# The first batch of an attention-into-MLP kernel in a new order: exponentials over two PSUM banks, strided pairs first, local V ahead of the next loads

## The chip, the cores and the metric

The kernel runs on one core of one Trainium2 chip. The metric is the device time of one execution in microseconds; lower is better. The engines named below are TensorE (PE, with its weight loads PEld), VectorE (DVE), ScalarE (ACT), GpSimd (POOL) and the DMA queues, of which SP issues the hardware ones and POOL the software ones.

## The reference

Inputs are q, k, v of shape (8 batches, 8 heads, 576 positions, 64), and two weights, 512x2048 and 2048x512. Everything is given and returned as float32.

```python
scores = scale * np.matmul(q, k.transpose(0, 1, 3, 2))
rel = pos[:, None] - pos[None, :]
mask_local = (rel >= 0) & (rel < 32)
mask_strided = (rel >= 0) & (pos[None, :] % 32 == pos[:, None] % 32)
# heads 0..3 use mask_local, heads 4..7 mask_strided
attn = softmax(where(mask, scores, -1e9))
x = (attn @ v) as (4608 tokens, 512)       # heads side by side
h = x @ w_in; g = relu(h) ** 2; out = g @ w_out
```

## The kernel before

Attention and MLP are one program, interleaved by hand. The result of the attention, transposed, lies in four tiles `xt[0..3]` of 128 features by 4608 tokens: `xt[0]` and `xt[1]` take the local heads, `xt[2]` and `xt[3]` the strided ones. The MLP goes over nine chunks of 512 tokens. For each chunk, `mm1` makes 16 blocks of 128 hidden features, four 128x512 matmuls each (L662), then a ReLU on ACT (L668) and a square on DVE one tick later (L669); `mm2` makes 16 groups of four matmuls for the output (L684), copied by ACT and stored.

The order is written out. `BATCH0` is a string of words, run once at the start; `PLAN` gives words to be run ahead of numbered groups, a group being one `mm1` or `mm2` step of about 0.86 us of PE. The letter says what a word does: `c` casts loaded q or k to bf16, `T` transposes it on PE and copies it out of PSUM (last letter: a for ACT, v for DVE, g for POOL), `W` transposes strided rows, `S` scores and exponentials, `N` sums, logarithm and exponential for the reciprocal of the sum, `O` the product with V and the normalising multiplication (L609 for strided units), `D` the product with V and the normalisation of local units (L627, L628), `E` their transposition into `xt` (L644, L647), `H` a copy that shifts the rows of local V, `w` matmuls on zeros whose result nobody reads (L719), `P` the first three `mm1` blocks, with the feature tiles named after it, `m` a memset, `l`, `r`, `U`, `V`, `o` loads issued by POOL, `s` and `x` the scores and products of later strided heads (L562 and L568 are their multiplications). Units 0 and 1 of a batch are the local pairs of heads, 2 and 3 the strided ones; `c5q` is the cast of q for unit 5, that is unit 1 of batch 1.

Within one engine everything runs in the order in which the words issue it. The first batch uses PSUM through a rotating list of seven banks (`banks["b0"]`), a score step four of them: two halves by two rows (heads). In the first batch the mask is added on PE: a matmul puts a bias into the bank (L482) and the scores are accumulated on it (L493). Each of the four banks has an exponential of its own (L503). `step_N` takes the logarithm of each half by itself (L585) and then the exponential of both (L586).

The loads at the start are unit 0's q and k on SP, and on POOL, in order: strided q, strided k (with the construction of the identity between them), unit 1's q and k (L291), local V (L404), strided V (L572), the four slices of `w_in` (L425). Those on POOL share one software queue.

Of the kernel before, what the change touches and what calls it, by code (L numbers as in the profile page):

```python
# [12 lines left out]

FIRST = (0, 2, 3, 1)
NP = 3
BATCH0 = """
    c0qv c0ka T0qa c1kg w2 T0kv S0 mk1v c1qv W0k0a w3 W0q0v W0k1a W0q1v T1qv w2 T1kv S2 S1 H0v D0.0 D0.1 S3
    D1.0 N3 D1.1 N2 E0a O3 O2 E1a w1 P0 P23 P1  # L20
"""
PLAN = """
0: l1q4+5 l1k4+5 z
1: r1q U1 mv1g
3: o0
4: r1k V1 mk0v
5: o1 l2k8+9 mbg
6: o2 o3 V2 mv0v
7: c4qv
8: c5qv  # L30
9: c4kv
10: l2q8+9 c5ka T4qa
11: T4kv T5qa
12: W1q0v T5ka
13: S4
14: W1q1v
16: W1k0a S5! B10v
17: W1k1a
18: D4.0 k10v mrg C2q C2k
19: k11v  # L40
20: D4.1 s1.0 B11v
21: D5.0 s1.1 U2
22: l3k12+13 s1.2
23: D5.1
24: E5v x1.0
26: X2k l3q12+13
27: E4v x1.1 c9kv
28: V3
29: x1.2 c8qv
30: c8ka c9qv  # L50
31: X2q
34: C3q B20v
35: T8kv B21v
37: T9kv
38: T8qv C3k
39: k20v
40: U3
41: S8! k21v
42: T9qa
44: S9! D8.0  # L60
46: D8.1
47: E8
# [101 lines left out]
def kernel(  # L164
# [41 lines left out]
    PS = bass.MemoryType.PSUM  # L206
    strTs = {nm: ctx.enter_context(tc.tile_pool(name=f"strT{nm}", bufs=n)) for nm, n in (("q", 2), ("k", 1))}
    psum = ctx.enter_context(tc.tile_pool(name="psum", bufs=1, space=PS))
    banks = {nm: [psum.tile([128, 512], FP32, name=f"{nm}{i}") for i in range(n)]
             for nm, n in (("ph", 2), ("py", 1), ("pt", 5))}  # L210

    banks["b0"] = banks["pt"] + banks["ph"]
    in_b0 = [True]

    def bank(nm):
        if in_b0[0] and nm == "pt":
            nm = "b0"
        t = banks[nm].pop(0)
        banks[nm].append(t)
        while id(t) in unread:  # L220
            run_due(lambda x: x[1] == unread[id(t)])
        return t

    unread = {}

# [219 lines left out]
        clock[0] += 1  # L445
        run_due(lambda x: x[0] <= clock[0])

    def step_T(u, name, copy):
        s = st[u]
        src = s[name].rearrange("p j h d -> p (j h d)")  # L450
        pt = bank("pt").bitcast(BF16)[:, 0:S]
        for j in range(6):
            nc.tensor.transpose(pt[:, QL * j:QL * (j + 1)], src[:, 128 * j:128 * (j + 1)],  # L453
                                ident[0:QL, 0:QL])
        if name == "k":
            full = kTl[v_slot(u)]
            dst = full[:, 32:32 + S]
        else:
            full = dst = qkT.tile([128, S], BF16, name="qT")
        copy(dst.rearrange("c (p j) -> c p j", j=6), pt.rearrange("c (j p) -> c p j", j=6))  # L460
        s[name + "T"] = full
# [4 lines left out]
    def step_S(u, mode=0):  # L466
        s = st[u]
        qT, kT = s["qT"], s["kT"]
        local = is_local(u)
        w, n = (QL, NL) if local else (SP_, NJ)  # L470
        kn = 128 if local else SP_
        hn = n // 2
        e = es[u % 4]
        s["e"] = e
        pss = [[None, None], [None, None]]
        for half in range(2):
            for row in range(2):
                pss[row][half] = bank("pt")
                if u < 4:
                    bias = bias_l[:, half].rearrange("p t c -> p (t c)") if local \  # L480
                        else bias_s.rearrange("p t c -> p (t c)")
                    nc.tensor.matmul(pss[row][half][0:kn, 0:S // 2], ident[0:kn, 0:kn], bias,  # L482
                                     start=True, stop=False, skip_group_check=True)
            for i in range(hn):
                t = half * hn + i
                klo = w * t
                for row in range(2):
                    rows = slice(64 * row, 64 * row + 64)
                    if not local:
                        lhsT, rhs = (a[rows, t // 4, t % 4, :] for a in (kT, qT))  # L490
                    else:
                        lhsT, rhs = kT[rows, klo:klo + kn], qT[rows, w * t:w * (t + 1)]
                    nc.tensor.matmul(pss[row][half][0:kn, w * i:w * (i + 1)], lhsT, rhs,  # L493
                                     start=u > 3, stop=True, skip_group_check=u < 4)

        for row in range(2):
            for half in range(2):
                unread[id(pss[row][half])] = u

        def expo(row, half):  # L500
            del unread[id(pss[row][half])]
            lo = S * row + S // 2 * half
            nc.scalar.activation(e[0:kn, lo:lo + S // 2], pss[row][half][0:kn, 0:S // 2],  # L503
                                 AF.Exp, scale=scale)

        def masks(row):
            x = e[0:kn, S * row:S * (row + 1)].rearrange("p (t c) -> p t c", c=w)
            m = mask_all if local else mask_str.to_broadcast([kn, n, w])
            nc.vector.tensor_tensor(x, x, m, op=ALU.mult)  # L509

        if u < 4:
            for half in range(2):
                for row in range(2):
                    expo(row, half)
            return
        if mode == 1:
            for row in range(2):
                for half in range(2):
                    expo(row, half)
                later(row + 1, lambda row=row: masks(row), u)  # L520
            return
        expo(0, 0)
        later(1, lambda: expo(0, 1), u)
        later(2, lambda: (masks(0), expo(1, 0)), u)
        later(3, lambda: expo(1, 1), u)
        later(4, lambda: masks(1), u)
# [17 lines left out]
    def step_XX(b, part):  # L544
# [11 lines left out]
        for h in (3,) if part == 2 else range(3):  # L556
            for par in range(2):
                r, x = slice(64 * par, 64 * par + 64), slice(64 * (h % 2), 64 * (h % 2) + 64)
                to = xt[2 + h // 2][x, b * S:(b + 1) * S].rearrange("c (m a r) -> c m a r", a=NP2, r=2)
                if part < 2:  # L560
                    of, by = (y[r, 0:W3 * n].rearrange("c (a h m) -> c h m a", a=n, h=3)[:, h] for y in (po, rv))
                    nc.vector.tensor_tensor(to[:, :, NJ * part:NJ * (part + 1), par], of, by, op=ALU.mult)  # L562
                    continue
                of, by = (y[r, 0:W3 * n].rearrange("c (a g m) -> c g m a", a=n, g=3) for y in (po, rv))
                for lo, g, k in ((0, 0, NG), (NG, 2, 1)):
                    t = to[:, :, 2 * NG * (g == 2) + lo, par]
                    t = bass.AP(t.tensor, t.offset, [t.ap[0], [2 * NG, 3 - g], [STRIDE, NA], [2, k]])
                    nc.vector.tensor_tensor(t, of[:, g:, :, lo:lo + k], by[:, g:, :, lo:lo + k], op=ALU.mult)  # L568

    def load_v0():  # L570
        load_v_local_sw(0)
        nc.gpsimd.dma_start(  # L572
            out=vs0.rearrange("p u n d -> p (u n d)").rearrange("p (h c) -> p h c", h=4),
            in_=v[0, 4:8].rearrange("h (p j) d -> p h (j d)", j=NJ))

    def step_N(u):
        e, hw = st[u]["e"], S // 2
        kn = 128 if is_local(u) else SP_
        for half in range(2):
            pn = bank("pt")  # L580
            for h in range(2):
                c = S * h + hw * half if is_local(u) else S * half + hw * h
                nc.tensor.matmul(pn[64 * h:64 * h + 64, 0:hw], ones[0:kn], e[0:kn, c:c + hw],
                                 start=True, stop=True)
            nc.scalar.activation(rv0[:, u, hw * half:hw * (half + 1)], pn[:, 0:hw], AF.Ln)  # L585
        nc.scalar.activation(rv0[:, u], rv0[:, u], AF.Exp, scale=-1.0)  # L586

    def step_O(u):
        s = st.pop(u)
        e, hw = s["e"], S // 2  # L590
        for half in range(2):
# [12 lines left out]
            for t in range(hw // w):  # L604
# [2 lines left out]
                    nc.tensor.matmul(po[64 * h:64 * h + 64, w * t:w * (t + 1)], vt, e[0:w, c:c + w],  # L607
                                     start=True, stop=True)
            nc.vector.tensor_tensor(  # L609
                xt[u][:, 0:S].rearrange("c (p j r) -> c p j r", j=NJ // 2, r=2)[:, :, :, half],  # L610
                po[:, 0:hw].rearrange("c (j p) -> c p j", p=SP_),
                rv.rearrange("c (j p) -> c p j", p=SP_), op=ALU.mult)

    def step_D(u, part):
        run_due(lambda x: x[1] == u)
# [105 lines left out]
    idle = xt[0][:, T - 512:T]  # L721

    def first_part(kks):
        in_b0[0] = False
        for ff in range(NP):
            mm1(0, ff, kks, FIRST, None if ff < 2 else "py")

    def run_step(word):
# [3 lines left out]
        elif op == "c":  # L732
            cast_qk_local(int(arg[:-2]), arg[-2], ENG[arg[-1]])
        elif op == "T":
            step_T(int(arg[:-2]), arg[-2], ENG[arg[-1]])
        elif op == "W":
            step_TS(int(arg[0]), arg[1], int(arg[2]), ENG[arg[3]])
        elif op == "S":
# [65 lines left out]
    def memset_later(which, eng):  # L804
# [5 lines left out]
        else:  # L810
# [3 lines left out]
    nc.scalar.preload_act_table_set("natural_log_exp_and_others")  # L814
    load_qk_hw(0)
    load_str_rows(0, "q")
    make_identity(nc, ident)
    load_str_rows(0, "k")
    nc.vector.memset(idle, 0.0)
    nc.vector.memset(mask_loc, 1.0)  # L820
    warm(8)
    nc.vector.memset(ones, 1.0)
    nc.vector.memset(kTl[0][:, 0:32], 0.0)
    nc.vector.memset(kTl[1][:, 0:32], 0.0)
# [19 lines left out]
    nc.vector.memset(bias_l[0:32, 0, 0], -NEG)  # L844
    nc.vector.tensor_scalar(bias_s, mask_str.to_broadcast([SP_, NJ // 2, SP_]),
                            NEG, -NEG, op0=ALU.mult, op1=ALU.add)
    load_qk_local_sw(0, (1,))
    load_v0()
    for i in range(4):
# [75 lines left out]
```

## Time and profile before

| | us |
|---|---|
| median of three runs (304.8 to 307.27) | 307.2 |
| the profiled execution | 307.11 |
| its span in the trace | 305.4 |
| PE busy | 297.6 (97%) |
| DVE busy | 179.7 (59%) |
| ACT busy | 173.2 (57%) |
| POOL busy | 73.3 (24%) |

Busy times are sums over the span; a busy PE is not PE at its peak. The lines of the span's first 60 us that the prediction works with stand there. Times in the trace start at the span's start.

### The profile page before, as it was taken

How to read it: one execution, taken by the hardware profiler on the slowest of the kernel's cores; microseconds unless marked ns; L12 is line 12 of the kernel's file. 1: busy time of each engine (PE TensorE's matmuls, PEld its weight loads, DVE VectorE, ACT ScalarE, POOL GpSimd, SP SyncE). 2: the span in 40 equal slices, each digit the busy share in tenths (PEclk: the TensorE clock that was granted, in tenths of full speed). 3: DMA queues.
4: the chain of work that ended last, by engine and by line, in shares of the span. 5: the costliest groups of instructions: out<-in, count | busy, mean ns of one | idle time of the engine just before them, and what ended most of it. 6: DMA issues, size and time to landing. Idle time of an engine off the chain costs nothing.

```text
span 305.4 us, 5745 instructions
## 1 busy us (share of the span) xinstructions
PE 297.6 (97%) x2177; PEld 147.8 (48%) x2177; DVE 179.7 (59%) x465; ACT 173.2 (57%) x342; POOL 73.3 (24%) x105
## 2 busy tenths in 40 slices
PE   7989899999999999999999999999999999999996
PEld 3554455455554544454445444444454444444444
DVE  4675777888578776575558394685576525104400
ACT  3395763768658754674477455744675446216611
POOL 8745835008131044066100840000000000000000
PEclk9999999999999999999999999999999999999999
DMA  8999999999989989599977998811110110010012
GB/s 149 184 206 195 188 201 189 161 202 138 144 137 205 134 156 188 125 151 150 199 123 125 136 181 175 118 21 71 69 23 19 71 70 0 34 71 34 0 69 71
DMA packets 93643, 37.28 MB, mean 122 GB/s; under 512 B 78956, under 2 KB 87750, under 8 KB 93616
## 3 DMA queue, kind: packets, MB, share of 16 engines
q0 software_dynamic: 54960, 18.82, 55.8%
q1 hardware_dynamic: 38512, 18.03, 29.7%
q8 instruction: 17, 0.28, 0.4%
q14 instruction: 10, 0.08, 0.1%
q10 hardware_dynamic: 144, 0.07, 0.1%
HBM read 38.21 MB, written 9.44 MB: 156 GB/s over the span
## 4 chain that ended last, share of the span: by engine, by line
PE 90%; DVE 5%; ACT 2%; issue 2%; POOL 0%; DVEq 0%; ACTq 0%; POOLq 0%
PE ph L662 38%; PE ph L684 36%; PE pt L493 2%; PE pt L622 2%; PE pt L453 2%; DVE xt L562 2%; PE pt L538 1%; PE pt L552 1%; PE ph L709 1%; PE pt L549 1%; PE py L719 1%; PE py L684 1%; DVE g_sb L669 1%; PE pt L482 1%; PE pt L684 1%
## 5 line engine op out<-in xcount | busy, mean ns | idle before, releaser
L662 PE MATMUL ph<-xt,w_in_b 128*128 128x512 bf16 x568 | 131.9, 379 | 1.1 <-ACT xt L647 0.8
L684 PE MATMUL ph<-w_out_b,g_sb 128*128 128x512 bf16 x528 | 121.1, 379 | 0.1
L668 ACT ACTIVATE r<-ph 128x512 bf16<-128x512 f32 x142 | 84.8, 599 | 35.2 <-PE ph L662 31.2
L669 DVE TENSOR_TENSOR g_sb<-r 128x512 bf16<-128x512 bf16 x144 | 60.5, 422 | 64.6 <-ACT r L668 63.8
L662 PEld LDWEIGHTS <-w_in_b 128*128 128x128 bf16 x576 | 53.0, 97 | 59.7 <-issue 2.3
L684 PEld LDWEIGHTS <-g_sb 128*128 128x128 bf16 x560 | 51.7, 98 | 57.4 <-DVE g_sb L669 0.5
L688 ACT COPY y<-ph 128x512 f32<-128x512 f32 x33 | 19.4, 589 | 53.1 <-PE ph L684 53.1
L562 DVE TENSOR_TENSOR xt<-pt,rv 64x144 bf16<-64x144 f32 x84 | 34.0, 405 | 18.4 <-ACT rv L555 17.3
L503 ACT ACTIVATE e<-pt 128x288 bf16<-128x288 f32 (+1 forms) x68 | 24.1, 417 | 8.7 <-PE pt L493 8.5
L554 ACT ACTIVATE rv<-pt 128x432 f32<-128x432 f32 (+1 forms) x21 | 10.5, 501 | 13.8 <-PE pt L549 13.8
L628 DVE TENSOR_TENSOR x_l<-pt,rinv 96x384 bf16<-96x384 f32 x30 | 16.6, 554 | 1.0
L568 DVE TENSOR_TENSOR xt<-pt,rv 64x270 bf16<-64x270 f32 (+1 forms) x28 | 10.9, 432 | 8.1 <-ACT rv L555 8.0
L350 POOL DMA_DIRECT2D q_t<-in_q_dram x6 | 3.5, 591 | 47.0 <-DMA qT_s<-q_t 47.0
L509 DVE TENSOR_TENSOR e<-e,mask_all 128x576 bf16<-128x576 bf16 x28 | 12.4, 453 | 3.9 <-ACT e L503 3.5
L539 ACT ACTIVATE e<-pt 128x432 bf16<-128x432 f32 (+1 forms) x21 | 10.4, 497 | 6.6 <-PE pt L538 6.6
L279 POOL DMA_DIRECT2D k_l<-in_k_dram x16 | 12.0, 759 | 2.2 <-DMA v_st<-in_v_dram 1.2
L279 POOL DMA_DIRECT2D q_l<-in_q_dram x16 | 11.7, 732 | 2.0 <-DMA k_l<-in_k_dram 1.3
L622 PEld LDWEIGHTS <-e 128*128 128x128 bf16 x192 | 9.1, 97 | 5.8 <-issue 0.4
L419 POOL DMA_DIRECT2D vl<-in_v_dram x7 | 10.0, 1436 | 6.3 <-DMA vl<-in_v_dram 2.7
L555 ACT ACTIVATE rv<-rv 128x432 f32<-128x432 f32 (+1 forms) x21 | 11.2, 533 | 0.7
L350 POOL DMA_DIRECT2D k_t<-in_k_dram x6 | 3.2, 539 | 29.8 <-DMA kT_s<-k_t 29.8
L622 PE MATMUL pt<-vl,e 128*128 128x65 bf16 x180 | 9.9, 193 | 0.0
(130 smaller groups left out, 223.5 us busy)
## 6 DMA issues: line engine op xcount, KB each, us to landing
out_dram<-y SPq DMA_DIRECT2D x35, 256.0 KB, 3.6
vl<-in_v_dram POOLq DMA_DIRECT2D x7, 384.0 KB, 9.4
w_in_b<-in_moe_w_in_dram POOLq DMA_DIRECT2D x4, 512.0 KB, 12.8
w_out_b<-in_moe_w_out_dram POOLq DMA_DIRECT2D x4, 512.0 KB, 13.9
q_t<-in_q_dram POOLq DMA_DIRECT2D x7, 288.0 KB, 6.8
k_t<-in_k_dram POOLq DMA_DIRECT2D x7, 288.0 KB, 5.9
v_st<-in_v_dram POOLq DMA_DIRECT2D x7, 216.0 KB, 7.5
k_l<-in_k_dram POOLq DMA_DIRECT2D x16, 72.0 KB, 6.7
```

Source lines behind the costliest of these rows:

```text
L279: nc.gpsimd.dma_start(out=t[:, :, hh, :], in_=src[b, 2 * p + hh].rearrange("(t p) d -> p t d", p=QL))
L503: nc.scalar.activation(e[0:kn, lo:lo + S // 2], pss[row][half][0:kn, 0:S // 2], AF.Exp, scale=scale)
L509: nc.vector.tensor_tensor(x, x, m, op=ALU.mult)
L555: nc.scalar.activation(rv, rv, AF.Exp, scale=-1.0)
L562: nc.vector.tensor_tensor(to[:, :, NJ * part:NJ * (part + 1), par], of, by, op=ALU.mult)
L622: nc.tensor.matmul(po[:, n, :], e[:, c:c + 128], rhs[:, NL * part + n, 0:D + 1], start=True, stop=True)
L628: nc.vector.tensor_tensor(x, po[0:QL, :, 0:D], rinv[0:QL].to_broadcast([QL, NL, D]), op=ALU.mult)
L662: nc.tensor.matmul(ph, w_in_b[:, kk, 128 * ff:128 * (ff + 1)], xt[kk][:, 512 * c:512 * (c + 1)], start=(kk == order[0]), stop=(kk == order ...
L668: nc.scalar.activation(r, ph, AF.Relu)
L669: later(1, lambda: nc.vector.tensor_tensor(g[:, ff, :], r, r, op=ALU.mult))
L684: nc.tensor.matmul(py, g[:, ff, 128 * j:128 * (j + 1)], w_out_b[:, ff, :], start=(ff == 0), stop=(ff == 15))
L688: nc.scalar.copy(y, py)
```

## The change

`BATCH0` is reordered. The strided units 2 and 3 are scored ahead of unit 1; unit 0's q is cast by ACT and its k by DVE; both casts of unit 1 are on DVE; the shift of local V is on POOL; unit 1's transposed k uses the bank that the spare matmuls use; unit 2's and unit 3's sums and products stand between the steps of units 0 and 1; there are ten spare matmuls at the start and 21 in all instead of 16; P takes feature tile 2 first and tiles 3 and 1 last (`FIRST`). The strided k load is issued ahead of the identity, local V ahead of unit 1's q and k. PSUM becomes one tile with eight slices, so that a score step in the first batch can take two neighbouring banks (`bank_pair`) and have one exponential over both rows of a half, and `step_N` one logarithm over both halves. In `PLAN` the words of batch 1 are moved, most by some groups; of the four memsets of the block tiles `kbds` and `vbds` (L812), one of `kbds`, so far on DVE in the first batch, is on POOL. The multiplications of `step_O` and `step_XX` go through their inputs in the order in which these lie, and write with the stride instead.

```diff
-FIRST = (0, 2, 3, 1)
+FIRST = (2, 0, 3, 1)
 BATCH0 = """
-    c0qv c0ka T0qa c1kg w2 T0kv S0 mk1v c1qv W0k0a w3 W0q0v W0k1a W0q1v T1qv w2 T1kv S2 S1 H0v D0.0 D0.1 S3
-    D1.0 N3 D1.1 N2 E0a O3 O2 E1a w1 P0 P23 P1
+    c0qa c0kv T0qa w1 T0kv w1 S0 W0q0v W0q1v w3 W0k0a W0k1v S2 H0g c1qv c1kv S3 T1qv w2 T1kvp D0.0 D0.1 N2 S1 O2 N3
+    E0a D1.0 D1.1 O3 w2 E1a w2 P2 P0 P31
 """
 PLAN = """
 0: l1q4+5 l1k4+5 z
-1: r1q U1 mv1g
+1: r1q U1 mk0v
+2: mk1g mv1g
 3: o0
-4: r1k V1 mk0v
-5: o1 l2k8+9 mbg
-6: o2 o3 V2 mv0v
-7: c4qv
-8: c5qv
-9: c4kv
-10: l2q8+9 c5ka T4qa
-11: T4kv T5qa
-12: W1q0v T5ka
-13: S4
-14: W1q1v
-16: W1k0a S5! B10v
-17: W1k1a
-18: D4.0 k10v mrg C2q C2k
-19: k11v
-20: D4.1 s1.0 B11v
-21: D5.0 s1.1 U2
-22: l3k12+13 s1.2
-23: D5.1
-24: E5v x1.0
-26: X2k l3q12+13
-27: E4v x1.1 c9kv
-28: V3
-29: x1.2 c8qv
+4: r1k o1 mv0v
+5: V1 mbg
+6: o2 o3
+7: l2k8+9 V2
+9: c4qv
+10: c5qv T4qa l2q8+9
+12: c4kv c5ka T5qa
+13: T4kv W1q0v
+14: T5ka W1q1v
+15: S4
+16: B10v
+17: W1k0a W1k1a
+18: S5!
+19: k10v mrg C2q C2k B11v
+20: k11v
+21: s1.0 U2
+22: s1.1 D4.0
+23: s1.2 D4.1 l3k12+13
+24: D5.0
+25: D5.1 x1.0
+26: E5v l3q12+13
+27: x1.1
+28: E4v V3
+30: x1.2 c9kv
...
-    banks = {nm: [psum.tile([128, 512], FP32, name=f"{nm}{i}") for i in range(n)]
-             for nm, n in (("ph", 2), ("py", 1), ("pt", 5))}
-
-    banks["b0"] = banks["pt"] + banks["ph"]
+    psb = psum.tile([128, 8, 512], FP32, name="psb")
+    all_banks = [psb[:, i] for i in range(8)]
+    banks = {"b0": all_banks[0:7], "py": all_banks[7:8], "ph": [], "pt": []}
...
+    def bank_pair():
+
+        order = [bank_no[id(t)] for t in banks["b0"]]
+        i = min(range(6), key=lambda i: max(order.index(i), order.index(i + 1)))
+        two = all_banks[i:i + 2]
+        banks["b0"] = [t for t in banks["b0"] if t is not two[0] and t is not two[1]] + two
+        return two, psb[:, i:i + 2]
...
+            if u < 4:
+                (pss[0][half], pss[1][half]), both = bank_pair()
...
+            if u < 4:
+                hw = S // 2
+                nc.scalar.activation(e[0:kn, 0:2 * S].rearrange("p (r c) -> p r c", r=2)[:, :, hw * half:hw * (half + 1)],
+                                     both[0:kn, :, 0:hw], AF.Exp, scale=scale)
+        if u < 4:
+            return
...
-        if u < 4:
-            for half in range(2):
-                for row in range(2):
-                    expo(row, half)
-            return
...
-                to = xt[2 + h // 2][x, b * S:(b + 1) * S].rearrange("c (m a r) -> c m a r", a=NP2, r=2)
+                to = xt[2 + h // 2][x, b * S:(b + 1) * S].rearrange("c (m a r) -> c a m r", a=NP2, r=2)
                 if part < 2:
-                    of, by = (y[r, 0:W3 * n].rearrange("c (a h m) -> c h m a", a=n, h=3)[:, h] for y in (po, rv))
-                    nc.vector.tensor_tensor(to[:, :, NJ * part:NJ * (part + 1), par], of, by, op=ALU.mult)
+                    of, by = (y[r, 0:W3 * n].rearrange("c (a h m) -> c h a m", a=n, h=3)[:, h] for y in (po, rv))
+                    nc.vector.tensor_tensor(to[:, NJ * part:NJ * (part + 1), :, par], of, by, op=ALU.mult)
...
     def load_v0():
-        load_v_local_sw(0)
         nc.gpsimd.dma_start(
...
-            nc.scalar.activation(rv0[:, u, hw * half:hw * (half + 1)], pn[:, 0:hw], AF.Ln)
+        r = rv0[:, u].rearrange("p (t c) -> p t c", t=2)
+        nc.scalar.activation(r, both[:, :, 0:hw], AF.Ln)
         nc.scalar.activation(rv0[:, u], rv0[:, u], AF.Exp, scale=-1.0)
...
-                xt[u][:, 0:S].rearrange("c (p j r) -> c p j r", j=NJ // 2, r=2)[:, :, :, half],
-                po[:, 0:hw].rearrange("c (j p) -> c p j", p=SP_),
-                rv.rearrange("c (j p) -> c p j", p=SP_), op=ALU.mult)
+                xt[u][:, 0:S].rearrange("c (p j r) -> c j p r", j=NJ // 2, r=2)[:, :, :, half],
+                po[:, 0:hw].rearrange("c (j p) -> c j p", p=SP_),
+                rv.rearrange("c (j p) -> c j p", p=SP_), op=ALU.mult)
...
     load_qk_hw(0)
     load_str_rows(0, "q")
+    load_str_rows(0, "k")
     make_identity(nc, ident)
-    load_str_rows(0, "k")
     nc.vector.memset(idle, 0.0)
     nc.vector.memset(mask_loc, 1.0)
-    warm(8)
+    warm(10)
...
+    load_v_local_sw(0)
     load_qk_local_sw(0, (1,))
     load_v0()
```

## The prediction

> **What bounds the kernel now.** I read the windows first, then the waits of PE, then the chain and the timeline of the first 35 us, then the DMA landings, last the groups by shape.
>
> ```profile
> 40.00:50.00 10.00, 9.50 (x107) 5.17 (x104) 7.79 (x22) 4.66 (x12) 4.52 (x7) 1.00 1.53 190
> 50.00:100.00 50.00, 49.74 (x414) 25.52 (x413) 38.96 (x100) 34.11 (x69) 13.14 (x18) 1.00 1.31 167
> 100.00:200.00 100.00, 100.00 (x722) 48.78 (x720) 66.00 (x171) 60.18 (x121) 28.99 (x39) 1.00 1.16 149
> ```
>
> Columns: window, length, then busy time of PE, PEld, DVE, ACT, POOL. From 60 us on PE lists no wait at all, so the matmuls alone set that stretch and nothing there can give or take. The rest is decided before 60 us:
>
> ```profile
> PE pt L453 <- DVE q_l L298: 1.7, 2, 1.1
> PE py L719 <- DVE xt L819: 1.3, 1, 1.3
> PE ph L662 <- ACT xt L647: 0.8, 1, 0.8
> PE pt L493 <- ACT e L503: 0.5, 1, 0.5
> ...
> PE ph L662 <- DVE xt L568: 0.2, 1, 0.2
> ```
>
> ```profile
> 20.52 0.61 ACT g_sb L585 x2
> ...
> 21.74 0.63 ACT xt L647
> 22.37 0.04 issue
> 22.41 0.59 PE ph L662 x2
> ...
> 28.43 1.23 DVE kb L812
> ...
> 30.51 1.23 DVE vb L812
> ...
> 32.02 0.31 DVE q_l L298
> 32.33 0.05 issue
> 32.38 0.43 PE pt L453 x6
> ```
>
> The first dense stage starts at 22.41, when ACT has copied unit 0's output (L647). Its 12 matmuls of P end at 25.06; I call this instant T. PE then runs without a break to 31.26, waits 1.1 us for the cast of batch 1's q on DVE, which is behind two memsets of 1.23 us and seven squares of r, loses 0.5 us at S5 and 0.2 us at 59.46. So the time is T plus a fixed amount of matmul work plus those stalls, and I sum changes of T and of the stalls.
>
> ```profile
> 9.57 0.66 PE L332 MATMUL ph<-ident,w_out_b 96*128 96x96 bf16 x6
> 13.96 0.42 PE L453 MATMUL pt<-ident,k_l 96*128 96x96 bf16 x6
> ```
>
> Two sets of six 96-column transposes: the later set takes two thirds. The 128x512 spare matmuls follow each other after 0.43 us up to 13.6, the dense ones after 0.215 from 22.4. PE ran at half rate until about 13.8, although the granted clock column shows 1.00. Its unbroken stretch 1.27 to 4.87 (3.6 us) did not bring the short durations; the one from 8.27 (5.5 us, gaps under 0.1) did.
>
> **The change, part by part.** Start: ten spare matmuls at 0.427 reach 5.54. ACT casts q at its landing (0.82+3.4=4.2, 0.83 us, ready 5.1), DVE casts k (landing 1.28+3.8=5.1, 0.49 us, ready 5.6), so both transposes follow without a gap, with one spare each, to about 7.2. That is 5.9 us unbroken, more than the 5.5 that sufficed, so I take the short durations from about 7 us. Moving the strided k load ahead of the identity's construction costs 0.73 us of POOL, covered by those spares. The Trainium skill ("TensorE: Matmul & The Clock Gate", Part 1) says that about 3.4 us of sustained work in a free-running window lifts the gate; the 3.6 us stretch that failed fits a window that began before it, and by this rule too the switch comes by about 8 us.
>
> Loads: local V (2304 pieces) now goes ahead of unit 1's q and k.
>
> ```profile
> w_out_b<-in_k_dram POOLq DMA_DIRECT2D x1, 288.0 KB, 6.7
> vl<-in_v_dram POOLq DMA_DIRECT2D x1, 288.0 KB, 8.3
> xt<-in_q_dram POOLq DMA_DIRECT2D x1, 144.0 KB, 6.0
> xt<-in_k_dram POOLq DMA_DIRECT2D x1, 144.0 KB, 6.0
> ```
>
> Last column: us from issue to landing. Before: strided k 2.74+6.7=9.4, q1 4.25+6.0=10.3, k1 4.91+6.0=10.9, V 5.53+8.3=13.8. One queue serves them in order, so V now lands near 9.4+2.9=12.3 and k1 last of the five: at 13.8 at the latest by this, or near 12.7, as the small pieces' long tail no longer ends the group. I take 13.3, and 12.6 for q1. V's shift moves from DVE (0.49 us) to POOL, where it waits for V; by POOL's 96x768 copy (0.82 us) it takes an estimated 1.4, ready by 13.8. Behind it on POOL are batch 1's loads (issued at 11.78, now about 13.8); their data were behind w_in's last slice anyway (9.8+15.5=25.3), so nothing is late. The memset of kb that POOL takes over from DVE (1.29) delays w_out's first load by about 0.7, hidden by the same queue.
>
> Strided pairs first: with the fast clock their transposes, scores and exponentials fill PE until about 12.8, so unit 1 waits only for its load. From there DVE is the chain, in its new order: cast of k1 0.4, two transposed copies 0.75 each, two normalisations of unit 0 (0.19+0.55, pitch 0.72) 1.45, which free the bank that O2 needs, O2's matmuls 0.5, two products, then a 0.3 wait for unit 1's matmuls, two normalisations 1.45, E1's transposes 0.4, two spares 0.43:
> 13.3+0.4+1.5+1.45+0.5+0.9+0.3+1.45+0.4+0.4 = 20.6; P's 12 matmuls 2.65 give T=23.3. P31 needs the ACT copy of E1 (20.3+0.65=20.95) and O3 (21.1), both before P2 and P0 end at 21.9. T gains 1.8.
>
> ```profile
> L562 DVE TENSOR_TENSOR xt<-pt,rv 64x144 bf16<-64x144 f32 x84 | 34.0, 405 | 18.4 <-ACT rv L555 17.3
> L628 DVE TENSOR_TENSOR x_l<-pt,rinv 96x384 bf16<-96x384 f32 x30 | 16.6, 554 | 1.0
> L609 DVE TENSOR_TENSOR xt<-pt,g_sb 128x288 bf16<-128x288 f32 x2 | 1.2, 642 | 0.0
> ```
>
> Products of O: reading with a stride 288 columns cost 0.64, while 384 columns read in order cost 0.55. In order I estimate 0.45 each (L628's slope), 0.9 for two; if the write, now 16 or 64 bytes apart, costs what the read saved, 1.3. L562 would go from 0.405 to about 0.3, on an engine that has slack later. The Trainium skill ("Advanced Engine Details and Errata", Memory Cachelines) charges every access that lands in another 16-byte line, writes not excepted; by it the products stay at 0.64 and the sum rises by 0.4.
>
> Exponentials over two banks: eight of 576 columns for sixteen of 0.417; 576 columns cost 0.63 in L647, so ACT saves 8x0.2=1.6, and 0.3 on the Ln pairs. If two banks cost like two instructions nothing is saved: ACT would deliver E1 near 21, still ahead of 21.9. Zero on the chain either way. The spares rise from 16 to 21; only the last two (0.43) are on the chain, in the sum.
>
> Batch 1: the two DVE memsets stay ahead of c4q, and the cast now stands behind nine squares instead of seven. From the same T: seven squares end the before's wait at T+7.3. Two more cost 0.7, and P31's order gives the first r 0.43 earlier, of which I count 0.3: T4q at T+7.7, so 0.4 worse. c4k stands behind the square of group 11, and T4k only one group later: r 0.6, square 0.4, cast 0.4 and 0.2 of latencies against 0.86+0.26 of matmul work: a new wait of 0.45. S5 meets its banks as before. x1.2 comes one group later, against shorter products: between 0 and 0.5 for chunk 1's start, I take 0.1.
>
> Sum: -1.8+0.4+0.45+0.1 = -0.85. The profiled execution took 307.1 (span 305.4 and 1.7 around it), as much as the median of 307.2; so 306.2.
>
> **The rivals.**
> - The head wins more: k1 lands at 12.7 (-0.6) and DVE keeps up in batch 1, so that T4q waits for nothing (-1.5, the wait left in my sum) and T4k hardly (-0.4). For it: the memsets start earlier, l1q has landed at 11.78+15.0=26.8. Against: DVE's backlog is in the chain row by row. 303.7.
> - The load order bites: k1's landing decides from 14.15 on, where the 0.85 is gone. If it lands where the group behind it landed before (6.7+8.5=15.2), T is 25.2 and the batch 1 waits remain: 308.1, slower than before. For it: V's pieces are the slowest kind in that queue. Against: its bytes are fewer than all that had landed by 13.8.
> - PE stays at half rate to 13.8, because transposes are too thin to count: S3 ends near 14.9, T1k's copy at 16.8 instead of 15.2, T=24.9: 307.8. Against: the stretch that did end it held 24 transposes.
> - The single tile for all banks makes PE wait for strangers, so that the change doesn't do what it says. The built program has fewer waits on PE (454 against 463), so this has little: a wait of 0.1 at each of 35 output copies would give 309.7.
> - The write penalty above: 306.6, inside my case.
>
> **How the numbers follow.** 1% (3.1 us) is about what a measurement of this kernel can tell from no change. My case 0.53 with the penalty inside it, the head's win 0.24, load order 0.1, half rate 0.1, strangers 0.03. Within 1% are mine, load order and half rate, less what their tails cross; faster by over 1% needs a little more than the first rival, and the lowest of the runs before, 304.8, shows that an execution can lie 2.4 lower unaided. Faster 0.27, same 0.66, slower 0.07. Range: down to the first rival, past it a little, up past load order: 303.3 to 308.6.
>
> **What would show it.** Right: six-transposes at 0.42 from about 7 us on; unit 1's casts on DVE waiting for their DMA at 12.6 and 13.3; P's first matmul at 20.6; T4q waiting about 1.5 for DVE and T4k about 0.45; L562 near 0.3; nothing waiting on PE after 60 us. Wrong: P later than 22, transposes at 0.66 up to 13, or a DMA as PE's releaser between 25 and 60 us.

## The result and the profile after

| | median, us | lowest to highest | profiled execution | span |
|---|---|---|---|---|
| before, same chip | 306.16 | 304.8 to 307.27 | 307.11 | 305.4 |
| after | 335.33 | 333.88 to 336.79 | 336.79 | 335.1 |

The changed kernel takes 1.0955 times as long (95% interval 1.0867 to 1.1043): 29 us slower, where I had forecast 306.2 and a range that ended at 308.6.

The windows of after, with the columns of those shown for before (window, length, busy time of PE, PEld, DVE, ACT and POOL, granted clock, DMA):

```profile
20.00:25.00 5.00, 4.36 (x24) 1.81 (x25) 3.84 (x5) 0.64 (x1) 2.35 (x3) 0.70 1.26 206
40.00:50.00 10.00, 9.33 (x104) 4.88 (x104) 6.37 (x17) 6.42 (x16) 5.19 (x8) 1.00 1.55 190
50.00:100.00 50.00, 42.48 (x346) 21.78 (x350) 41.86 (x84) 27.56 (x53) 12.40 (x17) 0.97 0.94 133
100.00:200.00 100.00, 93.16 (x665) 45.29 (x678) 77.83 (x160) 55.85 (x113) 30.47 (x42) 1.00 1.13 140
```

Before, PE was busy for 49.74 and for all of 100.00 us in the last two windows. Now it stands still for 7.5 and 6.8 us in them, and DVE has grown from 38.96 to 41.86 and from 66.00 to 77.83 although fewer instructions ran. Little of the loss is in the head that the change is mostly about: P's first matmul starts at 22.09, just past the 22 that the prediction names as a sign of being wrong, and T is 26.3 instead of 25.06 (with the old multiplications, in the first experiment, 23.1). That is 1.3 of the 29.7 us between the two spans. Most of the rest is in the stretch that I had called settled. PE's waits say for whom:

```profile
PE psb L513 <- DVE xt L583: 5.5, 2, 3.9
PE psb L683 <- DVE xt L589: 3.7, 2, 2.0
PE psb L665 <- DVE xt L583: 2.5, 1, 2.5
PE psb L570 <- DVE xt L583: 2.4, 1, 2.4
PE psb L705 <- DVE g_sb L690: 2.3, 1, 2.3
PE psb L470 <- DVE q_l L315: 1.8, 1, 1.8
```

L583 and L589 are the multiplications of `step_XX` (L562 and L568 in before). Groups by shape on DVE (busy us, mean ns of one, idle time ahead of them):

```profile
L583 DVE TENSOR_TENSOR xt<-psb,rv 64x144 bf16<-64x144 f32 x84 | 66.0, 785 | 17.7 <-ACT rv L576 16.5
L589 DVE TENSOR_TENSOR xt<-psb,rv 64x270 bf16<-64x270 f32 x14 | 18.7, 1339 | 0.8 <-ACT rv L576 0.6
...
L630 DVE TENSOR_TENSOR xt<-psb,g_sb 128x288 bf16<-128x288 f32 x4 | 5.5, 1554 | 0.5 <-ACT e L517 0.5
```

Before, the same three shapes took 405, 634 and 642 ns; the prediction shows the first and the last, and this is the second:

```profile
L568 DVE TENSOR_TENSOR xt<-pt,rv 64x270 bf16<-64x270 f32 x14 | 8.9, 634 | 8.1 <-ACT rv L555 8.0
```

The 84 products of 144 columns alone cost DVE 32 us more. One place in the timeline shows how that reaches PE. DVE in before, then DVE and PE in after:

```profile
54.93 2.52 DVE L562 TENSOR_TENSOR xt<-pt,rv 64x144 bf16<-64x144 f32 x6 [0.28 <-ACT rv L555]
```

```profile
54.79 4.76 DVE L583 TENSOR_TENSOR xt<-psb,rv 64x144 bf16<-64x144 f32 x6 [0.56 <-ACT rv L576]
59.60 0.64 PE L665 MATMUL psb<-ident,x_l 96*128 96x96 bf16 x6 [2.55 <-DVE xt L583]
```

Six products in a row hold DVE for 4.76 us (before, 2.52). PE's next transposes need a PSUM bank that those products still read, and PE waits 2.55 us. And they then run as a set of six in 0.64, the half-rate length, not 0.42: after the pause the clock has gone down. The 0.70 in the window from 20 to 25 us is another such stretch, behind waits of 0.42, 0.96 and 0.45 us. In the trace's clock records after is at half rate at 21.97–25.39, 59.52–62.93, 202.88–209.71 and 233.6–237.0, together 17.1 us, in which at most half, 8.5 us, is lost.

### The profile page after: what moved, and what is told of

The parts are those of the page before. It is cut to its first block, busy times and chain, and to the rows that moved or that the text cites. A ratio compares the mean times of both kernels' runs of the same rounds, so it can differ in the third digit from the quotient of the medians.

```text
span 335.1 us, 5696 instructions
## 1 busy us (share of the span) xinstructions
PE 303.3 (91%) x2143; PEld 148.6 (44%) x2182; DVE 223.1 (67%) x465; ACT 173.0 (52%) x331; POOL 76.0 (23%) x106
## 4 chain that ended last, share of the span: by engine, by line
PE 63%; DVE 24%; ACT 5%; issue 4%; DMA 2%; POOL 1%; DVEq 0%; ACTq 0%; POOLq 0%
PE psb L683 34%; PE psb L705 22%; DVE xt L583 14%; DVE xt L589 3%; DMA xt<-in_q_dram 2%; PE psb L643 2%; DVE g_sb L690 1%; PE psb L559 1%; ACT r L689 1%; PE psb L730 1%; ACT rv L576 1%; PE psb L513 1%; ACT rv L575 1%; DVE xt L630 1%; DVE vb L415 1%
## 5 line engine op out<-in xcount | busy, mean ns | idle before, releaser
L683 PE MATMUL psb<-xt,w_in_b 128*128 128x512 bf16 x556 | 134.0, 382 | 5.1 <-DVE xt L589 3.7
L705 PE MATMUL psb<-w_out_b,g_sb 128*128 128x512 bf16 x544 | 132.4, 391 | 3.3 <-DVE g_sb L690 2.3
L689 ACT ACTIVATE r<-psb 128x512 bf16<-128x512 f32 x144 | 85.8, 598 | 42.7 <-PE psb L683 38.2
L583 DVE TENSOR_TENSOR xt<-psb,rv 64x144 bf16<-64x144 f32 x84 | 66.0, 785 | 17.7 <-ACT rv L576 16.5
L709 ACT COPY y<-psb 128x512 f32<-128x512 f32 x35 | 20.6, 587 | 64.4 <-PE psb L705 64.4
L529 ACT ACTIVATE e<-psb 128x288 bf16<-128x288 f32 x56 | 20.2, 415 | 12.1 <-PE psb L513 12.0
L589 DVE TENSOR_TENSOR xt<-psb,rv 64x270 bf16<-64x270 f32 (+1 forms) x28 | 19.8, 891 | 0.8 <-ACT rv L576 0.6
L575 ACT ACTIVATE rv<-psb 128x432 f32<-128x432 f32 (+1 forms) x21 | 10.5, 502 | 16.3 <-PE psb L570 16.3
L649 DVE TENSOR_TENSOR x_l<-psb,rinv 96x384 bf16<-96x384 f32 x32 | 17.7, 554 | 1.1
L643 PE MATMUL psb<-vl,e 128*128 128x65 bf16 x192 | 10.8, 193 | 1.3 <-DVE e L535 1.2
```

Of the source, the lines that this page charges most:

```text
L575: nc.scalar.activation(rv, pn, AF.Ln)
L583: nc.vector.tensor_tensor(to[:, NJ * part:NJ * (part + 1), :, par], of, by, op=ALU.mult)
L589: nc.vector.tensor_tensor(t, of[:, g:, lo:lo + k], by[:, g:, lo:lo + k], op=ALU.mult)
L643: nc.tensor.matmul(po[:, n, :], e[:, c:c + 128], rhs[:, NL * part + n, 0:D + 1], start=True, stop=True)
L649: nc.vector.tensor_tensor(x, po[0:QL, :, 0:D], rinv[0:QL].to_broadcast([QL, NL, D]), op=ALU.mult)
L683: nc.tensor.matmul(ph, w_in_b[:, kk, 128 * ff:128 * (ff + 1)], xt[kk][:, 512 * c:512 * (c + 1)], start=(kk == order[0]), stop=(kk == order ...
```

## The experiments

The question is which part costs 29 us: the order of the multiplications, or anything else of the change (the moved `PLAN`, the single PSUM tile, the two-bank exponentials).

**The multiplications as before, the rest of the change kept.** Three statements go back to the old orders (L583, L589, L630):

```diff
-  to = xt[...].rearrange("c (m a r) -> c a m r", a=NP2, r=2)
+  to = xt[...].rearrange("c (m a r) -> c m a r", a=NP2, r=2)
...
-  of, by = (y[...].rearrange("c (a h m) -> c h a m", a=n, h=3)[:, h] for y in (po, rv))
-  nc.vector.tensor_tensor(to[:, NJ * part:NJ * (part + 1), :, par], of, by, op=ALU.mult)
+  of, by = (y[...].rearrange("c (a h m) -> c h m a", a=n, h=3)[:, h] for y in (po, rv))
+  nc.vector.tensor_tensor(to[:, :, NJ * part:NJ * (part + 1), par], of, by, op=ALU.mult)
...
-  xt[u][...].rearrange("c (p j r) -> c j p r", ...)[:, :, :, half], ... "c (j p) -> c j p" ...
+  xt[u][...].rearrange("c (p j r) -> c p j r", ...)[:, :, :, half], ... "c (j p) -> c p j" ...
```

> The changed kernel with only the multiplications of step_XX and step_O (L583, L589, L630) back in the order of before. Theory A (the stride of their writes makes them twice as long and DVE late): these lines return to about 0.405, 0.63 and 0.64 us, PE has no wait on L583 or L589, half-rate stretches of PE disappear, and the time is 305 to 307, ratio 0.99 to 1.005. Theory B (the single PSUM tile, the moved plan or the re-ordered batch 0 costs by itself): the time stays above 315.

Measured: 306.99 us (306.02 to 307.93), 1.0034 times before (1.0003 to 1.0065). The group and PE's waits in it:

```profile
L583 DVE TENSOR_TENSOR xt<-psb,rv 64x144 bf16<-64x144 f32 x84 | 34.0, 404 | 18.0 <-ACT rv L576 16.9
```

```profile
PE psb L470 <- DVE q_l L315: 1.4, 1, 1.4
...
PE psb L683 <- DVE xt L589: 0.5, 1, 0.5
```

Waits of 0.5 and 0.3 us on the products are left. The three orders are the whole loss. The rows of PE's waits add up to about 26 us in after and 6 here; with the 8.5 us at most from half rate (this kernel has no such stretch after its start) that is at most 28.5 of the 30.3 us between the two spans. The last 1.8 us or more are not accounted for.

**Each order alone, in the kernel before.** The new order of `step_XX` only, then that of `step_O` only (the lines above, the other way round).

> The kernel before with only step_XX's multiplications going through their inputs in order (as in the changed kernel). Theory A: L562 goes from 0.405 to about 0.785 us, DVE becomes late in each batch, and the time is 325 to 335. Theory B: the moved plan is needed for the loss, so the time stays under 312.

Measured: 331.28 us, 1.0829 times before (1.0774 to 1.0884).

```profile
L562 DVE TENSOR_TENSOR xt<-pt,rv 64x144 bf16<-64x144 f32 x84 | 66.1, 786 | 16.6 <-ACT rv L555 15.5
```

```profile
PE ph L662 <- DVE xt L568: 6.1, 2, 4.4
PE pt L493 <- DVE xt L562: 5.5, 2, 3.9
PE pt L549 <- DVE xt L562: 3.3, 2, 2.4
```

The same length and the same kind of waits without the new batch 0, `PLAN` or PSUM tile: `step_XX` makes some 26 of the 29 us.

> The kernel before with only step_O's multiplication of the strided units (four instructions) in the changed order. Theory A: each takes 1.55 instead of 0.64 us; O3 and O2 stand ahead of the last tiles of P, so P ends 3 to 4 us later, and with a stretch of PE at half rate behind the pause up to 1.7 more: 309 to 312. If the multiplications are covered: 305 to 307.

Measured: 309.25 us, 1.014 times before (1.0081 to 1.0199).

```profile
PE ph L662 <- DVE xt L609: 2.0, 2, 1.5
```

```profile
L609 DVE TENSOR_TENSOR xt<-pt,g_sb 128x288 bf16<-128x288 f32 x2 | 2.9, 1630 | 0.0
L609 DVE TENSOR_TENSOR xt<-ph,g_sb 128x288 bf16<-128x288 f32 x2 | 2.7, 1542 | 0.2 <-PE ph L607 0.2
```

`step_O` has only four of these products, but in the head, where P waits for their output; the longest wait is 1.5 us, and the clock records show half rate from 19.81 to 26.64. T is 26.95. The kernel with the order of `step_XX` alone has the same start, an early full rate as well and neither of the two in its head, and its T is 22.77. So the four products of the head cost some 4 us.

**What in the new order costs: the read or the write.** A kernel by itself that computes nothing of the reference: DVE multiplies 144 float32 columns of PSUM by 144 of SBUF into bf16, with the step between two written elements as the only difference.

```python
def w(step):
    return big[:, 0:step * N].rearrange("p (n s) -> p n s", s=step)[:, :, 0]

def rd(t):
    return t[:, 0:N].rearrange("p (a m) -> p m a", m=18)           # a step of 72 bytes
...
nc.vector.tensor_tensor(w(1), ps[:, 0:N], sb[:, 0:N], op=M)    # L46; L47 to L52: steps 2, 4, ... 64
...
nc.vector.tensor_tensor(wr(1), rd(ps), rd(sb), op=M)           # L53: both inputs read with a stride, written in order
# L56: SBUF's input alone with the stride; L57: PSUM's alone
```

> A small program by itself that computes nothing of the reference and stores zeros: 144-column products of a PSUM and an SBUF operand (float32) into bf16 on 64 partitions, with the write at steps of 1, 2, 4, 8, 16, 32 and 64 elements, then with strided reads, copies, bf16 inputs and ACT copies, four times each. Theory A: reads in order cost about 0.29 us up to some step, and from 16 bytes (8 elements) on about 0.78; strided reads with a small write step cost 0.405. If the write step were free, all of the first seven would take the same.

Groups by shape on DVE, in the order of their cost:

```profile
L52 DVE TENSOR_TENSOR big<-ps,sb 64x144 bf16<-64x144 f32 x4 | 3.2, 790 | 0.1
L49 DVE TENSOR_TENSOR big<-ps,sb 64x144 bf16<-64x144 f32 x4 | 3.1, 785 | 0.1
...
L51 DVE TENSOR_TENSOR big<-ps,sb 64x144 bf16<-64x144 f32 x4 | 3.1, 773 | 0.1
...
L48 DVE TENSOR_TENSOR big<-ps,sb 64x144 bf16<-64x144 f32 x4 | 1.9, 468 | 0.1
...
L53 DVE TENSOR_TENSOR big<-ps,sb 64x144 bf16<-64x144 f32 x4 | 1.5, 385 | 0.1
L56 DVE TENSOR_TENSOR big<-ps,sb 64x144 bf16<-64x144 f32 x4 | 1.5, 380 | 0.1
L47 DVE TENSOR_TENSOR big<-ps,sb 64x144 bf16<-64x144 f32 x4 | 1.2, 310 | 0.1
L46 DVE TENSOR_TENSOR big<-ps,sb 64x144 bf16<-64x144 f32 x4 | 1.2, 299 | 7.0 <-ACT big L67 6.9
...
L57 DVE TENSOR_TENSOR big<-ps,sb 64x144 bf16<-64x144 f32 x4 | 1.2, 298 | 0.1
```

| step of the write, bytes | 2 | 4 | 8 | 16 | 32 | 64 | 128 |
|---|---|---|---|---|---|---|---|
| us | 0.299 | 0.310 | 0.468 | 0.785 | 0.749 | 0.773 | 0.790 |

The strided read that the change removes costs 0.09 (0.385 against 0.299); the strided write that it adds costs 0.48. The read's price is all on the side of SBUF: with only that input strided the product takes 0.380, with only the PSUM input strided 0.298, as in order. Before wrote with a step of 4 bytes, which is nearly free (with strided reads as well, as in before, L54 took 0.385; the kernel has 0.405); after writes with 64 (`step_XX`) or 16 (`step_O`), where the cost has reached its ceiling. It is no matter of the PSUM input or of the multiplication: a bf16 copy out of SBUF goes from 0.190 to 0.471, a cast from PSUM from 0.299 to 0.772 at 64 bytes.

**Read and write both in order, in the kernel before.** The destination of `step_XX` becomes contiguous. The tokens of the strided heads come out permuted.

```diff
-  nc.vector.tensor_tensor(to[:, :, NJ * part:NJ * (part + 1), par], of, by, op=ALU.mult)
+  c0 = 2 * NJ * NA * part + NJ * NA * par
+  t = to[:, c0:c0 + NJ * NA].rearrange("c (a m) -> c a m", m=NA)
+  nc.vector.tensor_tensor(t, of, by, op=ALU.mult)
```

> The kernel before with step_XX's multiplications reading in order and also writing in order, so that the tokens of the strided heads come out permuted. Theory A (the write stride costs, the order of reading saves): L562 takes about 0.30 us, L568's 270 columns about 0.43, and the time is 303.8 to 307.3, as before. Theory B (going through these inputs in order is slow by itself): L562 stays near 0.785 and the time above 325.

Measured: 306.27 us, 0.9996 times before (0.9961 to 1.0032).

```profile
L564 DVE TENSOR_TENSOR xt<-pt,rv 64x144 bf16<-64x144 f32 x84 | 25.6, 305 | 20.7 <-ACT rv L555 19.6
L570 DVE TENSOR_TENSOR xt<-pt,rv 64x270 bf16<-64x270 f32 x14 | 6.1, 438 | 11.8 <-ACT rv L555 11.6
```

With the write out of the way the products take 0.305, the "about 0.3" of the prediction. It buys next to nothing: 8 us less on DVE in this one group, and no change of the median clear of noise, since before's products made PE wait only 0.2 us. Its ten runs lie at 303.9 to 304.3 and at 306.2 to 306.6, those of before at 304.4 to 305.7 and at 306.8 to 308.0; level by level that is a gain of 0.7 to 0.8 us by the medians. So the `step_XX` part of the change had less than 1 us to win there, even at the price that I gave it.

**The head.** Ten spare matmuls instead of eight, alone, in the kernel before (`-warm(8)`, `+warm(10)`); and the new batch 0, with old multiplications and the old `PLAN`, except that the memset of `kbds` that batch 0 no longer does goes to POOL:

```diff
 PLAN = """
-1: r1q U1 mk0v
-2: mk1g mv1g
+1: r1q U1 mk1g mv1g
 3: o0
-4: r1k o1 mv0v
+4: r1k V1 mk0v
...
```

> The kernel before with ten spare matmuls at the start instead of eight, nothing else. Its executions fall at two levels, 304.4 to 304.8 and 306.9 to 307.7. Theory A: the lower level is PE at full rate from about 4 to 6 us on, the upper at 13.8 as in the profile of before; ten spares leave no gap up to the first transposes, so all executions lie at 304.3 to 305.3. Theory B: the levels come from the loads; both stay.

> The changed kernel with the multiplications as before and with the PLAN of before (one memset of kb, which the new first batch no longer holds, on POOL at group 1). Theory A: the moved words of batch 1 cost about 1 us by T4q one group behind its cast, T4k and the later x1.2, so this takes 305.0 to 306.0, against 306.0 to 307.9 with the new plan. Theory B: the plan is neutral and the time stays at 306.3 to 307.3.

Measured: 304.70 us (304.46 to 305.9), 0.9974 times before (0.9949 to 0.9998), for the spares; 304.81 (304.20 to 307.21), just under the 305.0 that I had expected at least, and 0.998 times before (0.995 to 1.001), for the new batch 0. So the two heads are worth the same. Their first transposes, in the timeline of before's profiled execution and in that of the kernel with ten spares:

```profile
5.42 0.66 PE L453 MATMUL pt<-ident,q_l 96*128 96x96 bf16 x6 [0.55 <-DVE q_l L298]
```

```profile
5.44 0.43 PE L453 MATMUL pt<-ident,q_l 96*128 96x96 bf16 x6 [0.46 <-DVE q_l L298]
```

The same set takes 0.66 at half rate and 0.43 at full. Full rate begins at 4.09 here, at 13.83 in before, and T is 22.69 instead of 25.06. The new batch 0 has T at 23.0. Over the spares alone its reordering saves nothing. The spares do not hurry the clock in every execution: at 4.09 the ninth had not begun. The single-order kernels above have eight spares and before's start, and their full rate began at 4.33 and at 6.16. What the two more do, as far as the times tell, is that no run misses it: all 12 lie below 306, where 14 of 35 runs of before lie above 306.7. Only one of the 12 was traced, and in two other kernels with ten spares single runs still lie 3 us above the lowest (307.21 against 304.20 with the new batch 0, 306.20 against 303.32 in the next experiment); what those consist of is open.

The difference between this kernel and the first experiment, 304.81 against 306.99, is the moved `PLAN`: it costs 2.2 us by the medians, 1.1 by the spans of the two traces from T on (281.7 in the first experiment, 280.6 here, 280.3 in before). The rest of the 2.2 is not seen in these two traces.

**Ten spares, and the two memsets ahead of c4q on POOL.** From the wait that the prediction had found at T4q:

```diff
-4: r1k V1 mk0v
+4: r1k V1
...
-6: o2 o3 V2 mv0v
+6: o2 o3 V2 mk0g mv0g
...
-    warm(8)
+    warm(10)
```

> The kernel before with ten spares and with the two memsets of kb and vb in batch 1 (1.23 us each on DVE, ahead of c4q) moved to POOL behind the loads of group 6. Theory A: T4q's wait of 1.1 us goes and the rest stays: 303.1 to 304.0. Theory B: the wait moves, to POOL's later loads or to another cast: 304.3 or more.

Measured: 303.42 us (303.32 to 306.2), 0.995 times before (0.9919 to 0.9982), some 1.5 us less. Eight of its 12 runs, at 303.3 to 303.5, are faster than every run with the spares alone.

```profile
28.52 0.42 PE L453 MATMUL pt<-ident,q_l 96*128 96x96 bf16 x6
...
30.85 0.43 PE L453 MATMUL pt<-ident,k_l 96*128 96x96 bf16 x6 [1.04 <-DVE k_l L298]
```

The wait of 1.1 us at q's transposes is gone; 1.04 us has come back at k's, whose cast is now the late one: the median is in the range of theory A, but the trace shows what theory B said. The profiled execution, 304.56, is among the slower of this kernel, so what the 1.3 us between its median and that of the spares alone consists of is not seen in this trace.

## Why the prediction was wrong

**The step that failed** is the term for the products: "L562 would go from 0.405 to about 0.3, on an engine that has slack later", and for `step_O` "0.45 each", or 1.3 for two "if the write, now 16 or 64 bytes apart, costs what the read saved". They measured 0.785, 1.339 (the 270 columns of `step_XX`) and 1.554 each. So `step_XX`, for which the sum has no term at all, costs some 26 us by itself, and `step_O`, for which the sum allows 0.4 at most, some 4. The upper bound was the mistake: I had a row for the strided read and took its price for the write's, and no row that I showed priced a write with such a step. An end that no row reached had to be left open upwards. The rule that I weighed there, the Trainium skill's "Advanced Engine Details and Errata", Memory Cachelines, does speak against the change, and I turned it into 0.4 us. The traces agree with it in kind: from 16 bytes on, one element in each line, the cost no longer rises. They go further in one thing: the Trainium skill asks there for at least two hits on a line to absorb the latency, and two hits (8 bytes) were not enough, with 0.468 instead of 0.299.

**"On an engine that has slack later"** failed beside it. DVE was busy 59% of the span before and is at 67% now, so by the mean the slack is still there. But twelve products come in two bursts of 4.8 us, in a queue that also holds the casts, the squares and the copies out of PSUM that PE needs every 0.86 us. And "from 60 us on PE lists no wait at all, so ... nothing there can give or take" is half true: less than 1 us could be won there, as the run with both in order shows, but any engine behind PE can lose there.

**The steps that held**, read from the first experiment, which has them without the products:

| step | predicted | measured |
|---|---|---|
| P's first matmul | 20.6 | 20.52 |
| casts of unit 1 on DVE | 12.6, 13.3 | 12.40, 13.22 |
| shift of V on POOL | 1.4 | 1.24 |
| exponential of 576 columns, two banks | 0.63 | 0.645 |
| wait at T4q | 1.5 | 1.4 |
| wait at T4k | 0.45 | 0.29 |
| added from T on | 0.95 | 1.4 |
| time of the profiled execution | 306.2 | 306.47 (median 306.99) |

The first row owes something to chance: in this kernel the first two products of `step_O` take 1.22 us and not the 0.9 of the sum, and the wait of 0.3 behind them is not there.

The rival with strangers in the single tile fell: the kernel with the new batch 0, which has that tile, is no slower than the one with spares alone. Load order and half rate to 13.8 fell too, since k1 was there at 13.22 and full rate began at 4.51.

**One cause was read wrong though its number was right.** My −1.8 for T came out (25.06 to about 23.1), but I had put nearly all of the working on the reordered steps. The run with spares alone gets T to 22.69: it is the early full rate. The 35 runs of before lie at two levels, 21 from 304.4 to 305.7 and 14 from 306.8 to 308.0, and the profiled execution that my sum started from is at the upper one. The kernels with eight spares and before's start had full rate from 4.33, 6.16 and 13.27, and before itself in its one trace from 13.83. That its lower runs are those with an early rise fits all this; no trace of such a run of before was taken. The Trainium skill ("TensorE: Matmul & The Clock Gate", Part 1) says that the window which lifts the gate runs freely, so that the same kernel meets it at another place each time; the four numbers agree in that, but spread over 9.5 us, where the Trainium skill has 0.5 us either way for sustained work. So, by this reading, my gain of T was one that before already has in most of its executions.

## What to carry to other kernels

When an access pattern must be strided on one side, give the stride to the read: here it cost 30% of a product (at the one step measured, 72 bytes), and 160% on the write once elements were 16 bytes or more apart. Bound an unseen cost by a row of the same kind (a write by a write), and where there is none leave the end open and measure the instruction by itself. An engine's mean slack says nothing of a burst: hold the burst's length against the pitch at which the bounding engine needs that queue.

## What the runs showed of the hardware that was not expected

- A bf16 write of DVE with a step of 4 bytes costs 4% more than in order, of 8 bytes 57%, of 16 to 128 bytes 150% to 164%. ACT has such a cliff too: a copy of 144 columns from PSUM into bf16 took 0.272, 0.313, 0.787 and 0.776 us at 2, 4, 16 and 64 bytes.
- A pause of PE of 2 to 4 us can cost more than itself. At the waits of 2.55, 3.93 and 2.30 us in after begin stretches at half rate of 3.41, 6.83 and 3.41 us, the last 0.8 us behind the wait's end; at its waits of 2.04 and 2.39 us none begins.
- The same eight spare matmuls at the start were followed by full rate at 4.33 us in one kernel and at 13.83 us in another, with T at 22.77 and 25.06. The two levels of before's runs lie 2.5 us apart by their medians.
